# Attention in a hand-given order over head pairs, two heads next to each other on the PE array

## The chip, the cores and the metric

The kernel runs on one core of one Trainium2 chip. The core has five engines with queues of their own: PE (matmul, with its weight loads shown apart as PEld), DVE (vector), ACT (scalar functions), POOL and SP. SP and POOL issue most of the transfers; 16 DMA engines carry them out. The metric is the device time of one execution in microseconds (us), lower is better.

## The reference

Attention of 8 batches with 12 heads, 448 tokens and 64 columns a head; its output, 3584 tokens of 768 columns, goes through a mixture of 8 experts of which each keeps its 80 best tokens.

```python
# attention
rms = sqrt(mean(x * x, axis=-1, keepdims=True) + 1e-06)     # for q and for k
q_n, k_n = q / rms * g_q, k / rms * g_k
scores = 1/sqrt(64) * matmul(q_n, k_n.transpose(0, 1, 3, 2))
attn = exp(scores - max); attn = attn / (sum(attn, axis=-1) + 1e-09)
o = matmul(attn, v)                      # (8, 12, 448, 64) -> x (3584, 768)
# experts
logits = x @ w_gate                      # (3584, 8)
expert_idx = argmax(logits); gate_w = softmax(logits)[expert_idx]
for e in range(8):
    tok_idx = the 80 tokens of expert e with the largest gate_w
    h = maximum(x[tok_idx] @ w1[e], 0.0)                    # 768 -> 1024
    out[tok_idx] = gate_w[tok_idx, None] * (h @ w2[e])      # 1024 -> 768
```

All other rows of the output are zero.

## The kernel before

The kernel works on pairs of heads (`HP = 2`). For a pair q, k and v are loaded as four tiles of 112 tokens. Squares, their sums (L111, L114), a root on ACT (L117) and a reciprocal (L120) give the scale of each token; L127 and L130 apply it. Transposes on PE (L141, L143) put both heads' columns on the partitions, head 0 on 0 to 63 and head 1 on 64 to 127 (`qnT`, `knT`). Then the heads are taken one after the other. For each tile j of 112 keys a score matmul (L160) uses 64 rows of the array and ACT takes the exp (L163). Four AV matmuls (L168) accumulate in one PSUM tile `po`. `v_sb` has a 65th column of ones, so that row 64 of `po` is the sum of the exps. That row is copied (L172), moved to partition 0 by a transfer, spread over 64 partitions by POOL (L176), inverted (L177) and multiplied into the output (L179), which goes to DRAM as `xT_b`.

After each batch the gate reads `xT_b` back in four tiles of tokens (`gxT`), transposes it to tokens on partitions, casts it to bf16 and writes it to `xbf_scratch`; six matmuls (L202) make the logits, from which the score of each token for its expert goes to `S_sb`. The order of the instructions in this part is the scheduler's: the code above is written batch by batch, and the engines' queues come out interleaved.

At the end 10 rounds of three DVE instructions over 8 x 3584 (L240, L242, L246) find the 80 best tokens of each expert. For each expert POOL gathers their rows (L261), and loads w1 and w2 (L274, L278, 1536 KB each, two buffers); PE transposes (L269) and multiplies (L287, L299), and POOL scatters the result (L306). All of these transfers stand in POOL's queue. The output's 28 blocks of zeros are written by SP before anything is loaded (L74):

```python
    for i in range(N // 128):
        nc.sync.dma_start(out=out[i * 128:(i + 1) * 128, :], in_=zeros[:, :])
```

Of the kernel before, what the change touches and what calls it, by code (L numbers as in the profile page):

```python
# [14 lines left out]
U32 = mybir.dt.uint32  # L16


@with_exitstack
def kernel(  # L20
# [21 lines left out]

    ST = 112
    NT = S // ST
    HP = 2
    DC = DM // 128
    FC = F // 128

    xTd = [nc.dram_tensor(f"xT_b{b}", (DM, S), F32, kind="Internal").ap()
           for b in range(B)]  # L50
# [6 lines left out]
    ident = cpool.tile([128, 128], F32)  # L57
    make_identity(nc, ident[:, :])
    identb = cpool.tile([128, 128], BF16)
    nc.vector.tensor_copy(identb[:, :], ident[:, :])  # L60

    gq_sb = cpool.tile([D, 1], F32)
    gk_sb = cpool.tile([D, 1], F32)
    nc.sync.dma_start(out=gq_sb[:, :], in_=g_q[:, None])
    nc.sync.dma_start(out=gk_sb[:, :], in_=g_k[:, None])
    gqk = cpool.tile([HP * D, 1], F32)
    nc.vector.tensor_mul(gqk[:D, :], gq_sb[:, :], gk_sb[:, :])
    nc.vector.tensor_scalar_mul(gqk[:D, :], gqk[:D, :], 1.0 / math.sqrt(D))
    nc.gpsimd.tensor_copy(gqk[D:2 * D, :], gqk[:D, :])

    zeros = cpool.tile([128, DM], F32)
    nc.vector.memset(zeros[:, :], 0.0)
    for i in range(N // 128):
        nc.sync.dma_start(out=out[i * 128:(i + 1) * 128, :], in_=zeros[:, :])  # L74

    S_sb = cpool.tile([E, N], F32)
    wg_sb = cpool.tile([128, DC, E], F32)
    nc.sync.dma_start(out=wg_sb[:, :, :],
                      in_=moe_w_gate.rearrange("(c p) e -> p c e", p=128))

    with tc.tile_pool(name="attn_sb", bufs=3) as spool, \
         tc.tile_pool(name="attn_ps", bufs=2, space=bass.MemoryType.PSUM) as ppool, \
         tc.tile_pool(name="attn_tps", bufs=2, space=bass.MemoryType.PSUM) as tps, \
         tc.tile_pool(name="attn_big", bufs=2) as bpool, \
         tc.tile_pool(name="gate_sb", bufs=3) as gsb, \
         tc.tile_pool(name="gate_ps", bufs=2, space=bass.MemoryType.PSUM) as gps:

        def attention_batch(b):
            for hp in range(H // HP):
                h0 = hp * HP  # L90
                q_sb = spool.tile([ST, NT, HP, D], F32, tag="q", name="q_sb")
                k_sb = spool.tile([ST, NT, HP, D], F32, tag="k", name="k_sb")
                v_sb = spool.tile([ST, NT, HP, D + 1], F32, tag="v",
                                  name="v_sb")
                nc.gpsimd.memset(v_sb[:, :, :, :], 1.0)
                for hh in range(HP):
                    h = h0 + hh
                    nc.sync.dma_start(
                        out=q_sb[:, :, hh, :],
                        in_=q[b, h].rearrange("(t p) d -> p t d", p=ST))  # L100
                    nc.sync.dma_start(
                        out=k_sb[:, :, hh, :],
                        in_=k[b, h].rearrange("(t p) d -> p t d", p=ST))
                    nc.sync.dma_start(
                        out=v_sb[:, :, hh, :D],
                        in_=v[b, h].rearrange("(t p) d -> p t d", p=ST))

                def rms_scale(src, name):
                    sq = spool.tile([ST, NT, HP, D], F32, tag=name + "sq",
                                    name=name + "sq")  # L110
                    nc.vector.tensor_mul(sq[:], src[:], src[:])  # L111
                    ssq = spool.tile([ST, NT, HP], F32, tag=name + "ssq",
                                     name=name + "ssq")
                    nc.vector.reduce_sum(out=ssq[:], in_=sq[:], axis=AX.X)  # L114
                    nc.vector.tensor_scalar(ssq[:], ssq[:], 1.0 / D, 1e-6,
                                            op0=ALU.mult, op1=ALU.add)
                    nc.scalar.sqrt(ssq[:], ssq[:])  # L117
                    rstd = spool.tile([ST, NT, HP], F32, tag=name + "rstd",
                                      name=name + "rstd")
                    nc.vector.reciprocal(rstd[:], ssq[:])  # L120
                    return rstd

                q_rstd = rms_scale(q_sb, "q")
                k_rstd = rms_scale(k_sb, "k")
                for t in range(NT):
                    for hh in range(HP):
                        nc.vector.tensor_scalar(  # L127
                            q_sb[:, t, hh, :], q_sb[:, t, hh, :],
                            q_rstd[:, t, hh:hh + 1], None, op0=ALU.mult)
                        nc.vector.tensor_scalar(  # L130
                            k_sb[:, t, hh, :], k_sb[:, t, hh, :],
                            k_rstd[:, t, hh:hh + 1], None, op0=ALU.mult)

                qnT = bpool.tile([HP * D, S], F32, tag="qnT", name="qnT")
                knT = bpool.tile([HP * D, S], F32, tag="knT", name="knT")
                for t in range(NT):
                    pq = tps.tile([HP * D, ST], F32, space=bass.MemoryType.PSUM, tag="transp",
                                  name="pq")
                    pk = tps.tile([HP * D, ST], F32, space=bass.MemoryType.PSUM, tag="transp",
                                  name="pk")  # L140
                    nc.tensor.transpose(pq[:, :], q_sb[:, t, :, :],  # L141
                                        ident[:ST, :ST])
                    nc.tensor.transpose(pk[:, :], k_sb[:, t, :, :],  # L143
                                        ident[:ST, :ST])
                    nc.vector.tensor_scalar(qnT[:, t * ST:(t + 1) * ST],  # L145
                                            pq[:, :], gqk[:, :], None,
                                            op0=ALU.mult)
                    nc.vector.tensor_copy(knT[:, t * ST:(t + 1) * ST],  # L148
                                          pk[:, :])

                for hh in range(HP):
                    h = h0 + hh
                    qT_h = qnT[hh * D:(hh + 1) * D, :]
                    kT_h = knT[hh * D:(hh + 1) * D, :]
                    attnT = [bpool.tile([ST, S], F32, tag=f"attnT{j}",
                                        name=f"attnT{j}") for j in range(NT)]
                    for j in range(NT):
                        ps = ppool.tile([ST, S], F32, space=bass.MemoryType.PSUM,
                                        tag="score", name="ps")
# [5 lines left out]
                    po = ppool.tile([D + 1, S], F32, space=bass.MemoryType.PSUM, tag="outT",  # L165
                                    name="po")
                    for j in range(NT):
                        nc.tensor.matmul(po[:, :], v_sb[:, j, hh, :],  # L168
                                         attnT[j][:, :],
                                         start=(j == 0), stop=(j == NT - 1))  # L170
                    zrow = spool.tile([D + 1, S], F32, tag="zrow", name="zrow")
                    nc.vector.tensor_copy(zrow[D:D + 1, :], po[D:D + 1, :])  # L172
                    zrow0 = spool.tile([1, S], F32, tag="zrow0", name="zrow0")
                    nc.sync.dma_start(out=zrow0[:, :], in_=zrow[D:D + 1, :])
                    zb = spool.tile([D, S], F32, tag="zb", name="zb")
                    nc.gpsimd.partition_broadcast(zb[:, :], zrow0[:, :])  # L176
                    nc.vector.reciprocal(zb[:, :], zb[:, :])  # L177
                    xT = spool.tile([D, S], F32, tag="xT", name="xT")
                    nc.vector.tensor_mul(xT[:, :], po[:D, :], zb[:, :])  # L179
                    nc.sync.dma_start(out=xTd[b][h * D:(h + 1) * D, :],  # L180
                                      in_=xT[:, :])

        def gate_tile(b, ti, ntok):
            xT = gsb.tile([128, DC, 128], F32, tag="gxT", name="gxT")
            nc.sync.dma_start(
                out=xT[:, :, :ntok],
# [158 lines left out]
```

## Time and profile before

| | |
|---|---|
| runs shown | 1396.58, 1398.98, 1406.75 us (median 1398.98) |
| profiled execution, span | 1407.2 us |
| mean granted clock of TensorE in it | 0.772 of 2.4 GHz |
| busy in it | PE 1042.4, PEld 423.1, DVE 969.9, ACT 476.5, POOL 130.1 us |
| moved | 100.69 MB |

The profiled execution is one of the program on the chip; its span runs from the first to the last instruction. The busy times of engines overlap, and those of PE are modelled at their ends. The granted clock is 1.0 at 2.4 GHz and 0.5 at 1.2 GHz; values between are means over a stretch.

### The profile page before, as it was taken

The numbers are of one execution on the slowest core, as the hardware profiler recorded it, in microseconds if no ns is written. First come the engines' busy times: TensorE is split into PE (matmuls) and PEld (weight loads), VectorE is DVE, ScalarE is ACT, GpSimd is POOL, SyncE is SP. The second block draws the span as 40 slices with busy tenths as digits, with TensorE's granted clock in tenths as the row PEclk, the third lists the DMA queues.
The fourth block names the chain that finished last, engine by engine and source line by source line (L and its number), as shares of the span: only waits on it lengthen the run. The fifth ranks groups of instructions, "written<-read, shape, count | busy, mean of one in ns | idle before, by whom it ended". The sixth has DMA issues, their size and how long they took to land. (4 is left out here: it accounts for less than half of the span.)

```text
span 1407.2 us, 11745 instructions
## 1 busy us (share of the span) xinstructions
PE 1042.4 (74%) x3088; PEld 423.1 (30%) x3088; DVE 969.9 (69%) x2386; ACT 476.5 (34%) x758; POOL 130.1 (9%) x183
## 2 busy tenths in 40 slices
PE   0889899899989998999898899989997130004544
PEld 0333234333333433333333233333332120003433
DVE  0887777877598668868877887698685159992110
ACT  0453433553265335534543543365241000000100
POOL 0000000100011000100010010001000100002121
PEclk9987787887588678979888878889798555556666
DMA  9321232223123212312232123123200930006997
GB/s 334 75 47 36 50 81 58 52 67 68 33 53 73 62 30 53 93 43 53 46 84 56 41 49 94 42 53 79 56 20 14 187 54 0 0 0 124 175 185 139
DMA packets 216147, 100.69 MB, mean 72 GB/s; under 512 B 172944, under 2 KB 205712, under 8 KB 216080
## 3 DMA queue, kind: packets, MB, share of 16 engines
q1 hardware_dynamic: 200592, 71.82, 21.1%
q0 software_dynamic: 15488, 28.12, 10.8%
q8 instruction: 25, 0.41, 0.1%
q14 instruction: 42, 0.34, 0.1%
HBM read 95.39 MB, written 29.50 MB: 89 GB/s over the span
## 5 line engine op out<-in xcount | busy, mean ns | idle before, releaser
L160 PE MATMUL ps<-qnT,knT 64*112 64x448 f32 x768 | 424.8, 680 | 8.6 <-DVE qnT L145 4.0
L168 PE MATMUL po<-attnT,v_sb 112*65 112x448 f32 x768 | 400.1, 658 | 10.3 <-ACT attnT L163 10.3
L163 ACT ACTIVATE attnT<-ps 112x448 f32<-112x448 f32 x384 | 202.0, 542 | 358.3 <-PE ps L160 356.4
L177 DVE RECIPROCAL zb<-zb 64x448 f32<-64x448 f32 x96 | 281.7, 2934 | 9.0 <-POOL zb L176 9.0
L160 PEld LDWEIGHTS ps<-qnT,knT 64*112 64x112 f32 x768 | 135.1, 203 | 198.7 <-issue 116.4
L168 PEld LDWEIGHTS po<-attnT,v_sb 112*65 112x65 f32 x768 | 111.9, 163 | 253.6 <-issue 213.4
L163 ACT ACT_TABLE_LOAD x91 | 116.8, 1283 | 100.8 <-PE ps L160 99.7
L176 POOL PARTITION_BROADCAST zb<-zrow x96 | 73.9, 769 | 761.3 <-DMA zrow<-zrow 494.7
L172 DVE COPY zrow<-po 1x448 f32<-1x448 f32 x96 | 59.7, 622 | 106.1 <-PE po L168 104.6
L141 PE MATMUL pq<-ident,q_sb 112*128 112x112 f32 x192 | 62.4, 325 | 89.8 <-DVE qnT L145 50.7
L269 PE MATMUL pxt<-identb,xg 80*128 80x80 bf16 x48 | 8.4, 226 | 152.2 <-DMA xg<-xbf_scratch,idx_e 148.6
L117 ACT ACT_TABLE_LOAD x91 | 116.8, 1283 | 2.3 <-PEq L326 0.7
L196 DVE CAST xbf<-pt 128x128 bf16<-128x128 f32 (+1 forms) x192 | 48.3, 272 | 74.9 <-PE pt L193 47.8
L291 ACT ACTIVATE h_sb<-ph 128x80 bf16<-128x80 f32 x64 | 14.5, 237 | 230.3 <-PE ph L287 230.1
L130 DVE TENSOR_SCALAR k_sb<-k_sb,krstd 112x64 f32<-112x64 f32 x384 | 92.1, 274 | 0.2
L127 DVE TENSOR_SCALAR q_sb<-q_sb,qrstd 112x64 f32<-112x64 f32 x384 | 85.1, 263 | 0.2
L193 PE MATMUL pt<-ident,gxT 128*128 128x128 f32 (+1 forms) x192 | 54.6, 337 | 39.2 <-DVE xbf L196 25.7
L141 PEld LDWEIGHTS pq<-ident,q_sb 112*128 112x128 f32 x192 | 29.8, 155 | 154.1 <-DVE qnT L145 74.2
L145 DVE TENSOR_SCALAR qnT<-pq,gqk 128x112 f32<-128x112 f32 x192 | 61.1, 318 | 17.1 <-PE pq L141 13.6
L143 PE MATMUL pk<-ident,k_sb 112*128 112x112 f32 x192 | 59.0, 308 | 17.3 <-DVE knT L148 16.3
L302 DVE TENSOR_SCALAR yo<-py,gw_e 80x384 f32<-80x384 f32 x16 | 9.8, 612 | 85.6 <-PE py L299 83.5
L211 ACT ACTIVATE lex<-lex 128x8 f32<-128x8 f32 (+1 forms) x32 | 6.7, 209 | 171.6 <-DVE lex L209 171.5
(55 smaller groups left out, 808.9 us busy)
## 6 DMA issues: line engine op xcount, KB each, us to landing
w_sb<-in_moe_w_dram POOLq DMA_DIRECT2D x16, 1536.0 KB, 15.6
out_dram<-zeros SPq DMA_DIRECT2D x28, 384.0 KB, 4.0
q_sb<-in_q_dram SPq DMA_DIRECT2D x96, 112.0 KB, 2.6
k_sb<-in_k_dram SPq DMA_DIRECT2D x96, 112.0 KB, 2.7
v_sb<-in_v_dram SPq DMA_DIRECT2D x96, 112.0 KB, 2.5
xT_b<-xT SPq DMA_DIRECT2D x96, 112.0 KB, 2.2
gxT<-xT_b SPq DMA_DIRECT2D x24, 384.0 KB, 4.6
xbf_scratch<-xbf SPq DMA_DIRECT2D x144, 32.0 KB, 1.5
```

The costliest lines, as they stand in the source:

```text
L117: nc.scalar.sqrt(ssq[:], ssq[:])
L127: nc.vector.tensor_scalar(q_sb[:, t, hh, :], q_sb[:, t, hh, :], q_rstd[:, t, hh:hh + 1], None, op0=ALU.mult)
L130: nc.vector.tensor_scalar(k_sb[:, t, hh, :], k_sb[:, t, hh, :], k_rstd[:, t, hh:hh + 1], None, op0=ALU.mult)
L141: nc.tensor.transpose(pq[:, :], q_sb[:, t, :, :], ident[:ST, :ST])
L143: nc.tensor.transpose(pk[:, :], k_sb[:, t, :, :], ident[:ST, :ST])
L145: nc.vector.tensor_scalar(qnT[:, t * ST:(t + 1) * ST], pq[:, :], gqk[:, :], None, op0=ALU.mult)
L160: nc.tensor.matmul(ps[:, :], kT_h[:, j * ST:(j + 1) * ST], qT_h[:, :], start=True, stop=True)
L163: nc.scalar.activation(attnT[j][:, :], ps[:, :], AF.Exp)
L168: nc.tensor.matmul(po[:, :], v_sb[:, j, hh, :], attnT[j][:, :], start=(j == 0), stop=(j == NT - 1))
L172: nc.vector.tensor_copy(zrow[D:D + 1, :], po[D:D + 1, :])
L176: nc.gpsimd.partition_broadcast(zb[:, :], zrow0[:, :])
L177: nc.vector.reciprocal(zb[:, :], zb[:, :])
```

## The change

The 48 pairs of all batches become steps of one loop (`for n in range(-4, NP + 6)`), in an order that is written out by hand (`manual_schedule`) and is kept by every engine. In step n the scores of pair n, AV of pair n - 1, the transposes of pair n + 1, the normalisation of pair n + 2 and the squares of pair n + 3 stand interleaved. The two heads' matmuls of a key tile stand next to each other: scores on rows 0 to 63 and 64 to 127, AV on columns 0 to 63 and 64 to 127 of one accumulator `po` (one buffer). The exp takes both heads at once. The column of ones goes; DVE adds the four exp tiles (`presum`), and for every second pair `zl` multiplies the sums with a selector and the unnormalised outputs `us` with the gate's weights, into one PSUM bank for a batch: 32 columns of the array for each of four heads. Some steps later `gate1`, `gate2` and `xout` transpose, divide, and write `xbf_scratch` once a batch; `xT_b` and its way through DRAM are gone. Square moves to ACT, the root becomes a power on POOL. The zero blocks are written in the loop, one for every second step. The weights of experts 0 and 1 are loaded in the loop; those of experts 2 to 6 have buffers of their own, in space that the attention's pools had, and expert 7 takes expert 2's. The expert loop keeps its matmuls; PSUM is read in larger pieces, and a gather has three buffers.

```diff
-                        nc.tensor.matmul(ps[:, :],
-                                         kT_h[:, j * ST:(j + 1) * ST],
-                                         qT_h[:, :], start=True, stop=True)
-                        nc.scalar.activation(attnT[j][:, :], ps[:, :], AF.Exp)
...
+        def square(n):
+            sq = prep.tile([ST, 2 * 2 * NT * D], F32, tag="sq", name="sq", bufs=1)
+            nc.scalar.activation(sq[:, :], st[n]["qk"][:].rearrange("p a h x -> p (a h x)"),
+                                 AF.Square)
...
+        def rstd(n):
+            ssq = prep.tile([ST, 16], F32, tag="ssq", name="ssq")
+            nc.vector.reduce_sum(out=ssq[:, :], in_=st[n]["sq"][:].rearrange(
+                "p (g d) -> p g d", d=D), axis=AX.X)
...
+            nc.gpsimd.tensor_tensor(rs[:].rearrange("p a h j -> p (a h j)"), ms[:, :],
+                                    nhalf[:, :], op=ALU.pow)
...
+        def transp(n, a):
+            tp = tpps.tile([128, 512], F32, tag="tp", name="tp")
+            for j in range(NT):
+                nc.tensor.transpose(tp[:, j * ST:(j + 1) * ST],
+                                    st[n]["qn"][:, a, j].rearrange("p h d -> p (h d)"),
+                                    ident[:ST, :ST])
...
+        def score(n, j):
...
+            ps = scps.tile([ST, 2, 512], F32, tag="sc", name="ps")
+            for hh in range(2):
+                nc.tensor.matmul(ps[:, hh, :S],
+                                 st[n]["T1"][hh * D:(hh + 1) * D, j * ST:(j + 1) * ST],
+                                 st[n]["T0"][hh * D:(hh + 1) * D, :],
+                                 start=True, stop=True)
+            nc.scalar.activation(st[n]["at"][:, j], ps[:, :, :S], AF.Exp)
+
+        def av(n, j):
+            if j == 0:
+                st[n]["po"] = pops.tile([128, 512], F32, tag="po", name="po")
+            for hh in range(2):
+                nc.tensor.matmul(st[n]["po"][hh * D:(hh + 1) * D, :S],
+                                 st[n]["v"][:, hh, j * D:(j + 1) * D],
+                                 st[n]["at"][:, j, hh, :],
+                                 start=(j == 0), stop=(j == NT - 1))
...
+        def presum(n):
...
+            nc.vector.tensor_add(t0[:], at[:, 0], at[:, 1])
+            nc.vector.tensor_add(t1[:], at[:, 2], at[:, 3])
+            nc.vector.tensor_add(sm[:], t0[:], t1[:])
...
+        def uevac(n):
+            us = upool.tile([128, S], F32, tag="us", name="us")
+            nc.vector.tensor_copy(us[:, :], st[n]["po"][:, :S])
...
+        def zl(n):
...
+                nc.tensor.matmul(t[32 * c:32 * c + 32, :S], zsel[:, i, :],
+                                 st[m]["sm"][:, c % 2, :], start=(i == 0), stop=False)
...
+                nc.tensor.matmul(t[32 * c:32 * c + 32, :S], wgs[:, 4 * i + c, :],
+                                 st[m]["us"][:, :], start=False, stop=(i == NG - 1))
...
+        for n in range(-4, NP + 6):
+            if ok(n + 4):
+                load_qk(n + 4)
+            if ok(n + 2):
+                load_v(n + 2)
+            if n >= 0 and n % 2 == 0 and n // 2 < N // 128:
+                i = n // 2
+                nc.sync.dma_start(out=out[i * 128:(i + 1) * 128, :], in_=zeros[:, :])
+            if n >= 2 and n % 6 == 2 and n // 6 < NW0:
+                fetch_w1(n // 6)
...
+            if ok(n):
+                score(n, 0)
+            if ok(n - 2):
+                uevac(n - 2)
+            if ok(n - 1):
+                av(n - 1, 0)
+                presum(n - 1)
+            if ok(n + 1):
+                transp(n + 1, 0)
+            if ok(n):
+                score(n, 1)
+            if ok(n - 1):
+                av(n - 1, 1)
+            if ok(n - 2) and (n - 2) % 2 == 1:
+                zl(n - 2)
+            if ok(n + 2):
+                normalise(n + 2)
...
+            if ok(n + 3):
+                square(n + 3)
+                rstd(n + 3)
+            if ok(n - 1):
+                av(n - 1, 3)
...
+        for e in range(NW0, E):
+            load_weights(wlate, e)
+            fetch_w1(e)
+            fetch_w2(e)
         for e in range(E):
```

PE's queue of the kernel before, in the middle of the attention; `ps` are the scores of one head, `po` its AV, `pq` and `pk` the transposes.

```order
L160 MATMUL ps<-qnT,knT 112x448 x2
L168 MATMUL po<-attnT_5847,v_sb 65x448
L168 MATMUL po<-attnT_5848,v_sb 65x448
L168 MATMUL po<-attnT_5849,v_sb 65x448
L168 MATMUL po<-attnT_5850,v_sb 65x448
L160 MATMUL ps<-qnT,knT 112x448 x2
L141 MATMUL pq<-ident,q_sb 128x112
L143 MATMUL pk<-ident,k_sb 128x112
```

PE's queue of the changed kernel for one pair with `zl`; each x2 of L189 (scores) and L199 (AV) is the two heads of a key tile.

```order
L189 MATMUL ps<-qkT 112x448 x2
L199 MATMUL po<-at,vt 64x448 x2
L174 MATMUL tp<-ident,qn 128x112 x4
L189 MATMUL ps<-qkT 112x448 x2
L199 MATMUL po<-at,vt 64x448 x2
L228 MATMUL zl<-sm,zsel 32x448 x4
L232 MATMUL zl<-us,wgs 32x448 x4
L189 MATMUL ps<-qkT 112x448 x2
L199 MATMUL po<-at,vt 64x448 x2
L174 MATMUL tp<-ident,qn 128x112 x4
L189 MATMUL ps<-qkT 112x448 x2
L199 MATMUL po<-at,vt 64x448 x2
```

Runs of one head's matmuls have become an alternation of score and AV, each for two heads.

DVE's queue of the changed kernel, from one copy of `po` (L216) to the next.

```order
L216 COPY us<-po 128x448
L209 TENSOR_TENSOR t_2784<-at 112x896
L210 TENSOR_TENSOR t_2785<-at 112x896
L211 TENSOR_TENSOR sm<-t_2784,t_2785 112x896 [waits DVE_49]
L165 TENSOR_TENSOR qn<-qk,rs 112x2x4x64 [waits DMAHW5_49,Pool_49]
L165 TENSOR_TENSOR qn<-qk,rs 112x2x4x64 [waits DMAHW6_49]
L151 TENSOR_REDUCE ssq<-sq 112x16 [waits Activation_49]
L289 TENSOR_TENSOR xb<-xp,rz 112x4x128 [waits PE_49] x2
L216 COPY us<-po 128x448
```

In DVE's queue of the kernel before, a head's row of sums and output are handled between other heads' work.

```order
L177 RECIPROCAL zb<-zb 64x448 [waits Pool_49]
L196 CAST xbf<-pt 128x128 [waits DMAHW1_49,PE_49]
L196 CAST xbf<-pt 128x128 [waits DMAHW2_49,PE_49]
L179 TENSOR_TENSOR xT<-po,zb 64x448 [waits DVE_49]
L196 CAST xbf<-pt 128x128 [waits DMAHW3_49,PE_49]
```

The reciprocals over 448 columns are gone, and the reduce L151, which waits for ACT's Square, now stands between the copies of `po`.

POOL's queue of the kernel before, from the last broadcast on; L274 and L278 load weights, L261 gathers, L306 scatters.

```order
L176 ISA zb<-zrow_7903 64x448
L274 DMA w_sb<-in_moe_w_dram 128x6x1024
L278 DMA w_sb<-in_moe_w_dram 128x8x768
L274 DMA w_sb<-in_moe_w_dram 128x6x1024
L278 DMA w_sb<-in_moe_w_dram 128x8x768
L261 DMA xg<-xbf_scratch,idx_e 80x768 x2
L274 DMA w_sb<-in_moe_w_dram 128x6x1024
```

POOL's queue of the changed kernel at its end; L102 and L106 load weights, L392 gathers, L426 scatters.

```order
L106 DMA w_sb<-in_moe_w_dram 128x8x768
L102 DMA w_sb<-in_moe_w_dram 128x6x1024 [waits DMASW4_49]
L106 DMA w_sb<-in_moe_w_dram 128x8x768 [waits DMASW5_49]
L392 DMA xg<-xbf_scratch,idx_e 80x768 [waits DMAHW0_49,DMASW6_49,DVE_49]
L392 DMA xg<-xbf_scratch,idx_e 80x768 [waits DMAHW2_49,DMASW7_49,DVE_49]
L392 DMA xg<-xbf_scratch,idx_e 80x768 [waits DMAHW4_49,DMASW0_49,DVE_49]
```

Ten weight loads (experts 2 to 6) now stand ahead of the first gather, where four stood; four others (experts 0 and 1) have moved into the attention.

## Rows read from the trace of the kernel before

**Rows 1.** Stages: us, busy PE, PEld, DVE, ACT, POOL (count), clock, DMA share, GB/s.

```profile
0.00:44.00 44.00, 2.52 (x8) 1.42 (x8) 9.85 (x39) 2.27 (x5) 2.40 (x10) 1.00 0.88 298
44.00:1082.00 1038.00, 949.49 (x2437) 359.45 (x2438) 804.34 (x2157) 458.47 (x686) 97.02 (x140) 0.82 0.24 55
1082.00:1148.40 66.40, 23.06 (x84) 14.19 (x82) 19.09 (x58) 1.26 (x5) 4.47 (x5) 0.54 0.69 130
1148.40:1264.40 116.00, 0.00 (x0) 0.00 (x0) 115.30 (x71) 0.00 (x0) 0.00 (x0) 0.50 0.00 0
1264.40:1407.20 142.80, 67.36 (x560) 48.08 (x560) 21.35 (x65) 14.46 (x64) 26.22 (x28) 0.66 0.84 154
```

**Rows 2.** Groups of 44 to 1082 us: busy us, mean ns, idle before.

```profile
L160 PE MATMUL ps<-qnT,knT 64*112 64x448 f32 x768 | 424.8, 680 | 8.6 <-DVE qnT L145 4.0 <-ACT attnT L163 3.5
L168 PE MATMUL po<-attnT,v_sb 112*65 112x448 f32 x761 | 397.5, 659 | 10.3 <-ACT attnT L163 10.3
L177 DVE RECIPROCAL zb<-zb 64x448 f32<-64x448 f32 x95 | 278.7, 2934 | 7.0 <-POOL zb L176 7.0
L163 ACT ACTIVATE attnT<-ps 112x448 f32<-112x448 f32 x384 | 202.0, 542 | 358.3 <-PE ps L160 356.4
...
L172 DVE COPY zrow<-po 1x448 f32<-1x448 f32 x95 | 59.1, 622 | 105.7 <-PE po L168 104.2
...
L111 DVE TENSOR_TENSOR ksq<-k_sb 112x512 f32<-112x512 f32 x47 | 32.0, 681 | 0.0
L114 DVE TENSOR_REDUCE kssq<-ksq 112x8 f32<-112x512 f32 x47 | 31.5, 670 | 0.2
...
L117 ACT ACTIVATE kssq<-kssq 112x8 f32<-112x8 f32 x47 | 9.8, 208 | 3.6 <-DVE kssq L115 3.2
```

**Rows 3.** Timeline of PEld, full clock: start us, us, instruction, idle before.

```profile
1080.84 0.27 PEld L160 LDWEIGHTS ps<-qnT,knT 64*112 64x112 f32 x2 [0.48 <-ACT attnT L163]
1081.77 0.19 PEld L168 LDWEIGHTS po<-attnT,v_sb 112*65 112x65 f32 x2 [0.66 <-PE ps L160]
1082.20 0.14 PEld L168 LDWEIGHTS po<-attnT,v_sb 112*65 112x65 f32 x1 [0.24 <-issue]
1082.58 0.14 PEld L168 LDWEIGHTS po<-attnT,v_sb 112*65 112x65 f32 x1 [0.24 <-issue]
```

**Rows 4.** Timeline of PEld at the lower clock.

```profile
424.32 0.23 PEld L168 LDWEIGHTS po<-attnT,v_sb 112*65 112x65 f32 x1 [0.51 <-issue]
425.07 0.23 PEld L168 LDWEIGHTS po<-attnT,v_sb 112*65 112x65 f32 x1 [0.52 <-issue]
```

**Rows 5.** Timeline of PE, two transposes.

```profile
440.82 0.26 PE L141 MATMUL pq<-ident,q_sb 112*128 112x112 f32 x1
440.92 0.26 PE L143 MATMUL pk<-ident,k_sb 112*128 112x112 f32 x1
```

**Rows 6.** Two stretches of 4 us, columns as in rows 1.

```profile
412.00:416.00 4.00, 1.11 (x4) 0.72 (x4) 3.73 (x9) 0.21 (x2) 0.86 (x2) 0.81 0.36 82
416.00:420.00 4.00, 3.73 (x7) 1.35 (x6) 4.00 (x9) 1.64 (x2) 0.24 (x1) 0.50 0.53 121
```

**Rows 7.** Timeline of SP's queue, the first load of q.

```profile
29.51 1.19 SPq L98 DMA_DIRECT2D q_sb<-in_q_dram  x1
```

**Rows 8.** Timeline of PEld, the drain.

```profile
1097.89 0.29 PEld L193 LDWEIGHTS pt<-ident,gxT 128*128 128x128 f32 x2 [13.67 <-DMA gxT<-xT_b]
```

**Rows 9.** Experts: transfers (KB, median us to landing), a stretch, two rows of PE.

```profile
idx_e<-idx_scratch SPq DMA_DIRECT2D x8, 0.3 KB, 5.1
out_dram<-yo,idx_e POOLq DMA_INDIRECT x8, 8.3
...
1278.00:1394.00 116.00, 56.66 (x485) 40.79 (x484) 14.88 (x53) 12.78 (x57) 23.29 (x25) 0.68 1.02 184
...
1280.13 0.24 PE L269 MATMUL pxt<-identb,xg 80*128 80x80 bf16 x2
...
1283.94 2.44 PE L299 MATMUL py<-w_sb,h_sb 128*80 128x384 bf16 x14
```

More of the change, by code (lines that the diff above doesn't have):

```diff
@@ L44 @@
     NT = S // ST
-    HP = 2
+    HP = H // 2
+    NP = B * HP
     DC = DM // 128
     FC = F // 128
-    xTd = [nc.dram_tensor(f"xT_b{b}", (DM, S), F32, kind="Internal").ap()
-           for b in range(B)]
+    NG = H // 4
     xbf_dram = nc.dram_tensor("xbf_scratch", (N, DM), BF16, kind="Internal").ap()
@@ L66 @@
[L66 to L71, printed above, removed]
-    nc.vector.memset(zeros[:, :], 0.0)
[L73 to L77, printed above, removed]
@@ new lines @@
+    gk2 = cpool.tile([128, 2], F32, name="gk2")
+    for half in range(2):
+        nc.sync.dma_start(out=gk2[half * D:(half + 1) * D, 0:1], in_=g_q[:, None])
+        nc.sync.dma_start(out=gk2[half * D:(half + 1) * D, 1:2], in_=g_k[:, None])
+    gqk = cpool.tile([128, 1], F32, name="gqk")
+    nc.vector.tensor_mul(gqk[:, :], gk2[:, 0:1], gk2[:, 1:2])
+    nc.vector.tensor_scalar_mul(gqk[:, :], gqk[:, :], 1.0 / math.sqrt(D))
+    zsel = cpool.tile([ST, NG, 32], F32, name="zsel")
+    nc.vector.memset(zsel[:, :, :], 0.0)
@@ new lines @@
+    for i in range(NG):
+        nc.vector.memset(zsel[:, i, 24 + i:25 + i], 1.0)
+    wgs = cpool.tile([128, H, 32], F32, name="wgs")
+    nc.vector.memset(wgs[:, :, :], 0.0)
+    wg_v = moe_w_gate.rearrange("(i c hh d) e -> hh d i c e", hh=2, c=2, d=D)
+    for hh in range(2):
+        for i in range(NG):
+            nc.sync.dma_start(
+                out=wgs[hh * D:(hh + 1) * D, 4 * i + hh:4 * i + hh + 3:2, 8 * i:8 * i + 8],
+                in_=wg_v[hh, :, i])
+    nhalf = cpool.tile([ST, 16], F32, name="nhalf")
@@ L283 @@
-            for fc in range(FC):
-                ph = mps.tile([128, CAP], F32, space=bass.MemoryType.PSUM, tag="ph",
-                              name="ph")
-                for c in range(DC):
-                    nc.tensor.matmul(ph[:, :],
-                                     w1_sb[:, c, fc * 128:(fc + 1) * 128],
-                                     xgT[:, c, :],
-                                     start=(c == 0), stop=(c == DC - 1))
-                nc.scalar.activation(h_sb[:, fc, :], ph[:, :], AF.Relu)
+                out=xg[:, :], out_offset=None, in_=xbf_dram[:, :],
@@ new lines @@
+            h_sb = mpool.tile([128, FC, CAP], BF16, tag="hsb", name="h_sb")
+            for fh in range(2):
+                ph = mps.tile([128, FC // 2, CAP], F32, tag="ph", name="ph")
+                for f4 in range(FC // 2):
+                    fc = fh * (FC // 2) + f4
+                    for c in range(DC):
+                        nc.tensor.matmul(ph[:, f4, :],
+                                         w1_sb[:, c, fc * 128:(fc + 1) * 128],
+                                         xgT[:, c, :],
+                                         start=(c == 0), stop=(c == DC - 1))
+                nc.scalar.activation(h_sb[:, fh * (FC // 2):(fh + 1) * (FC // 2), :],
+                                     ph[:], AF.Relu)
```

387 lines of the change are left out of this document (201 added, 186 removed).

## The prediction

> **What bounds the kernel now.** I read the stages first. Their rows [rows 1] cut the 1407.2 us of the profiled execution into a head without matmuls to speak of (44 us), the attention (1038 us for 48 pairs of heads, 21.6 us a pair), a drain with the last batch's gate (66 us), the top-k passes (116 us) and the experts (143 us). In the attention PE is busy 949 of 1038 us, DVE 804, ACT 458, so PE is the bound there, with DVE close behind. In the drain and the top-k no matmul matters, and in the experts the DMA share is 0.84 with PE at 67 of 143 us. So the attention must be priced in PE passes, the other stages by what ends last in each.
>
> The groups of the attention [rows 2] say what the passes are: scores 768 and AV 768 (two passes for each of the 384 matmuls), 825 of 949 us busy. The count is per head: a head uses 64 rows of the array for a score and 65 columns for AV. Because "busy" overlaps in a pipeline, I take the price of a pass from starts of weight loads instead. In a run of AV passes at full clock they start 0.376 us apart, 1082.20 to 1082.58 [rows 3]. Where a score pair is followed by AV the two passes take 0.93 us, 1080.84 to 1081.77, so a change of the form of the matmul costs 0.18 there; the first AV pass takes 0.43, or 0.05 more. At the lower clock, 1.2 GHz, a pass takes 0.75 us [rows 4]. Transposes of 112 columns start 0.10 us apart [rows 5]. The mean granted clock of the attention is 0.82 [rows 1]. It falls where PE has stood idle: in 412 to 416 us PE is busy 1.11 of 4 us, and in the four us behind it the clock is 0.50 though PE is busy 3.73 of 4 [rows 6].
>
> **The change, part by part.** *Scores and AV.* A pair still has 8 score and 8 AV matmuls of two passes and 448 columns, but the two heads of a step now stand next to each other, on rows 0 to 63 and 64 to 127 for scores, and on columns 0 to 63 and 64 to 127 for AV. No place of the trace of before has two matmuls on different tiles next to each other, so the price of such a pair must be bounded: two slots if both run fully side by side, four if not at all. I take three. PE issues in program order, first head pass 1, pass 2, second head pass 1, pass 2; pass 2 of a head needs the same rows as its pass 1, so it starts one slot later [rows 3], and only the second head's pass 1 can lie beside it. That is nearest to the one fact shown, that passes on the same rows follow each other at 0.376. Then a score step costs 3 x 0.376 + 0.18 = 1.31 us and a pair 5.2; an AV step, with a change that I put at 0.14 (between 0.05 and 0.18), 1.27 and a pair 5.1.
>
> *Transposes.* 8 a pair as before, in two blocks of 4: 0.8 us by [rows 5] and 0.2 for each change of form, 1.2. *Row sums and gate logits.* The 65th column of ones goes, as do the per-head RECIPROCAL of 2934 ns, its broadcast and the copy of a row [rows 2]. Instead there are 8 matmuls for two pairs, 32 columns of the array each. By the same staggering 16 passes take 9 slots, 3.4 us, so 1.75 a pair. The 4 output transposes of a pair take 0.5. Sum on PE: 5.2 + 5.1 + 1.2 + 1.75 + 0.5 = 13.8 us a pair at full clock. At the clock of before, 0.82, that is 16.8.
>
> *Waits between engines.* There is one AV accumulator, so the first AV step of a pair waits until DVE has copied out the last one. On DVE that copy stands behind the reduce of squares, which waits for the Square on ACT, which stands behind the last exp. From the end of the last score step the chain is: an exp of 896 columns, 0.88 us (542 ns for 448 and 208 for 8 give 0.75 ns a column [rows 2]); a Square of 1024 columns, 0.98 at the same rate; a reduce of 1024 elements, under twice the 670 ns of 512, 1.2; a copy of 448 columns, 0.62; about 0.2 for hand-overs: 3.9 us. Against it PE has one AV and one score step, 2.6 us. The stall is 1.3 us a pair at full clock and nothing at 1.2 GHz, where PE takes 5.1; I count 0.7. It could be 0, if the gate's work between two pairs covers it, or 1.3. The gate of a batch adds some ten short DVE instructions and six multiplications of 512 columns at about 0.68 [rows 2], some 6 us a batch, 1 us a pair; nothing if hidden, 1.3 if not at all. A pair: 16.8 + 0.7 + 1.0 = 18.5 us, the attention 48 x 18.5 = 888.
>
> *DVE and ACT* are not the bound: DVE has per pair three additions of 896 columns (1.2 each, by 681 for 512), two multiplications (0.7), the reduce (1.2) and the copy (0.6), 6.8 us; ACT four exps, two copies of 448 (0.54) and the Square, 5.6. If PE shared fully, they would still be under its 10 us.
>
> *Head.* The 28 zero fills leave the front of SP's queue, where the first load of q is issued at 29.51 [rows 7] and the first score at 44.0. Ten small transfers stay ahead of it; at 1.19 us each, as the row shows for q's issue, they would take 12, and I take half: 6 + 14.5 = 20 us in place of 44. The fills now go out one for every two pairs, between loads needed three to four pairs later; the DMA share there is 0.24 [rows 1], so I cost them, and the four weight loads of experts 0 and 1 that POOL issues there, at nothing. If that cover were gone, four loads at 8 us would cost 32.
>
> *Drain.* The way through DRAM goes: PE waits 13.67 us for its first tile [rows 8], and PE is busy only 23 of 66 us [rows 1]. What is left behind the last score is AV of the last pair (5.1 / 0.82 = 6), its sums and logits (3.4 / 0.82 = 4), and the gate's ten short DVE instructions and six multiplications with their hand-overs (an estimate, 12): 22 in place of 66. *Top-k.* 29 of 30 passes over 3584 columns remain: 116 x 29 / 30 = 112.
>
> *Experts.* Here the change costs time. Before, four weight loads were underway before the top-k; 12 followed. Now four are done in the attention, but the other loads stand on POOL ahead of the gathers, and their buffers are those of the attention's pools, so the first waits until the top-k has ended and the index writes have landed (4 us, under the 5.1 of the read back [rows 9]). A load is 1536 KB, which at 184 to 206 GB/s (the row 1278 to 1394 gives 184 [rows 9]) is 7.6 to 8.5 us; I take 8. The ten loads end 84 us behind the top-k; only then come the gathers, and PE, which had two experts' weights all along, begins at 87. An expert takes 6.3 us (1280.13 to 1283.94 + 2.44 [rows 9]). Expert 2's first half ends at about 103 and frees the buffer of expert 7's weights, 16 us more, 119; the gather of expert 4 stands behind these on POOL, 122; four experts, 25, and the last scatter's landing, 8.3 [rows 9]: 155 in place of 143.
>
> **Sum.** 20 + 888 + 22 + 112 + 155 = 1197 us against the span of 1407.2. The median of the runs shown, 1398.98, is 0.6% under that span, so 1197 becomes **1190**.
>
> **The rivals.**
> *Full sharing:* the two heads of a step run side by side in two slots. For it: rows and columns are disjoint. Against: two passes of each, issued in order. A pair: score steps 0.93 and AV steps 0.89, 7.3; transposes 1.2, sums 0.8, output 0.5: 9.8, at 0.82 12.0, with the gate 1.0 and the stall, now longer, 1.6: 14.6 x 48 = 701, plus 309: 1010, about 1005. The Trainium skill, "TensorE: Matmul & The Clock Gate", section "Measured speedup vs the span model", gives the span of packed tiles as about that of one matmul with a few ns for each further tile; by that rule this rival is the time. No run here shows it.
> *No sharing,* the change doing not what it says: 4 slots a step, 6.7 + 6.6 + 1.2 + 3.0 + 0.5 = 18.1. At full clock with gate and stall 19.7 a pair, 946 + 309, about 1250; at 0.82 23.3, about 1420; in the middle 1330. For it: nothing in the trace shows two tiles at work at once.
> *Full clock with sharing:* 13.8 + 1.3 + 1.0 = 16.1 a pair, 773 + 309, about 1075. For it: the order leaves PE fewer and shorter waits. Against: a stall of 1.3 us a pair stays, and the clock of before fell behind waits [rows 6].
> *The clock stays at 1.2 GHz:* short waits at every pair and the changes of form keep it down. A pass then takes 0.75 [rows 4], a pair 27.4 + 1.0, the attention 1363, the whole about 1660, slower than before. It decides where 13.8 / clock + 1.7 passes (1407 - 309) / 48 = 22.9 us, at a mean clock under 0.65. For it: drain and experts of before ran at 0.50 to 0.66 [rows 1]. Against: the attention, with longer waits than those to come, kept 0.82.
>
> **How the numbers follow.** Chances: the forecast with sharing in three slots and a clock near 0.82, 0.45; full sharing 0.15; full clock 0.12; no sharing 0.20, a quarter of it slower than before; the low clock 0.08. The forecast alone, with its bounds (stall 0 to 1.3, gate 0 to 1.3, clock 0.78 to 0.88, experts 143 to 165), spans 1130 to 1250. For 8 in 10 the range takes in the full-clock case, half of the full sharing and most of no sharing: 1020 to 1400; outside are the low clock and the ends, together under 0.2. A change within 1%, which is about what a measurement of this kernel can tell from none, needs one narrow stretch of the no-sharing case: 0.03. Slower by over 1%: 0.08 + 0.04 = 0.12. Faster: 0.85.
>
> **What the profile after would show.** Right: in a score step the weight loads of the four passes start so that the step takes 1.3 us at full clock, not 0.9 or 1.7; 18 to 19 us a pair; a wait of about 1 us of the first AV step for DVE's copy; first score at about 20 us; a MoE stage that is longer than before, with PE idle for some 85 us behind the top-k while weights come. I would be wrong if steps take two or four slots, if the clock of the attention leaves 0.78 to 0.88, if the gathers pass the weight loads in the queue, or if DVE, not PE, sets the pace.

## The result and the profile after

The changed kernel takes 963.2 us (962.13 to 969.48, four runs) against 1399.62 for the kernel before: the ratio is 0.6877, 95% interval 0.6842 to 0.6913. The forecast was 1190 with a range from 1020; the kernel is faster than the whole range. The profiled execution has a span of 960.3 us at a mean clock of 0.803.

The stages of the changed kernel, columns as in [rows 1]: head, attention (first to last score), drain, top-k, experts.

```profile
0.00:21.50 21.50, 1.75 (x8) 1.41 (x8) 5.40 (x14) 4.58 (x6) 4.33 (x10) 1.00 0.35 83
21.50:676.40 654.90, 537.03 (x2488) 179.19 (x2488) 340.07 (x467) 274.87 (x339) 150.69 (x97) 0.88 0.29 82
676.40:694.25 17.85, 11.82 (x68) 6.07 (x64) 12.88 (x25) 0.76 (x2) 0.00 (x0) 0.81 0.00 0
694.25:809.00 114.75, 0.00 (x0) 0.00 (x0) 113.79 (x50) 0.00 (x0) 0.00 (x0) 0.50 0.03 9
809.00:960.30 151.30, 43.64 (x560) 34.22 (x560) 16.02 (x36) 7.00 (x16) 25.92 (x28) 0.66 0.77 145
```

Four of the five stages came out near their terms: 21.5 (forecast 20), 17.9 (22), 114.8 (112) and 151.3 (155), together 305 for 309. The error lies in the attention: 655 us, 13.6 a pair, for 888. The groups of its 655 us answer to [rows 2]; the last number before an arrow is the engine's idle time ahead of the group:

```profile
L189 PE MATMUL ps<-qkT 64*112 64x448 f32 x768 | 224.4, 666 | 0.6 <-ACT qkT L181 0.6
L199 PE MATMUL po<-at,vt 112*64 112x448 f32 x752 | 202.6, 619 | 64.1 <-DVE us L216 34.3 <-issue 25.6 <-PE ps L189 4.2
L193 ACT ACTIVATE at<-ps 112x896 f32<-112x896 f32 x192 | 176.1, 917 | 231.8 <-PE ps L189 231.8
...
L151 DVE TENSOR_REDUCE ssq<-sq 112x16 f32<-112x1024 f32 x46 | 56.1, 1220 | 270.4 <-ACT sq L145 270.4
...
L145 ACT ACTIVATE sq<-qk 112x1024 f32<-112x1024 f32 x46 | 48.3, 1049 | 0.0
...
L276 PE MATMUL sp<-ident,sc 112*8 112x112 f32 x28 | 6.4, 381 | 30.9 <-DVE sc L273 30.9
L240 PE MATMUL zt<-ident,zsb 128*112 128x128 f32 x28 | 4.5, 285 | 19.9 <-DVE zsb L237 19.9
```

The counts of passes are those of before (768 and 768, some records missing), but the busy time has halved: 224 for 425 us, 203 for 398. Weight loads of the changed kernel, as in [rows 3], show one score step, one AV step and one block of transposes:

```profile
409.72 0.27 PEld L189 LDWEIGHTS ps<-qkT 64*112 64x112 f32 x4 [0.70 <-issue]
410.66 0.20 PEld L199 LDWEIGHTS po<-at,vt 112*64 112x64 f32 x4 [0.67 <-issue]
411.56 0.39 PEld L174 LDWEIGHTS tp<-ident,qn 112*128 112x128 f32 x4 [0.70 <-issue]
```

A score step takes 0.94 us and an AV step 0.90: two slots (a slot is the 0.376 us of one pass) and a change of form each, not three slots. Inside the score step the four weight loads lie within 0.27 us.

PE is idle for 118 of the 655 us, in the places that were named: 64.1 ahead of AV and 51 ahead of the gate's transposes (L276, L240). The timeline of PE at the first AV step of a pair, that of DVE ahead of it, and two stretches of 4 us around it:

```profile
401.71 1.01 PE L189 MATMUL ps<-qkT 64*112 64x448 f32 x4
404.86 1.55 PE L199 MATMUL po<-at,vt 112*64 112x448 f32 x4 [2.14 <-issue]
406.34 1.01 PE L174 MATMUL tp<-ident,qn 112*128 112x112 f32 x4
407.28 1.61 PE L189 MATMUL ps<-qkT 64*112 64x448 f32 x4
```

```profile
401.81 1.22 DVE L151 TENSOR_REDUCE ssq<-sq 112x16 f32<-112x1024 f32 x1 [6.32 <-ACT sq L145]
402.94 1.28 DVE L289 TENSOR_TENSOR xb<-xp,rz 112x512 bf16<-112x512 f32 x2
404.14 0.61 DVE L216 COPY us<-po 128x448 f32<-128x448 f32 x1
```

```profile
401.00:405.00 4.00, 1.86 (x14) 0.98 (x13) 3.19 (x5) 1.69 (x2) 1.80 (x2) 1.00 0.00 0
405.00:409.00 4.00, 4.00 (x14) 1.36 (x14) 3.96 (x5) 0.70 (x2) 1.30 (x1) 0.57 0.00 0
```

AV waits 2.14 us, and behind the wait the granted clock is 0.57: the next score step takes 1.5 us instead of 0.94. The wait is put down to "issue", but DVE's copy L216 ran from 404.14 to 404.75, just ahead of AV's start at 404.86. Two of the gate's multiplications (L289) stand between the reduce and the copy here and make 1.28 us of the chain.

In the experts' stage POOL's timeline has the first weight load and the first gather, and PE's the first matmul:

```profile
811.61 0.89 POOL L102 DMA_DIRECT2D w_sb<-in_moe_w_dram  x1 [168.89 <-DMA gw_scratch<-gw_all]
...
839.22 1.06 POOL L392 DMA_INDIRECT xg<-xbf_scratch,idx_e  x1 [7.13 <-DMA w_sb<-in_moe_w_dram]
...
891.31 0.96 PE L398 MATMUL pxt<-identb,xg 80*128 80x80 bf16 x12 [197.70 <-DMA xg<-xbf_scratch,idx_e]
```

The gather is issued at 839.22, but PE gets its rows only at 891.31, 82 us behind the end of the top-k, when the loads ahead of it are in (forecast 87).

### The profile page after: what moved, and what is told of

Read it like the earlier page. It is cut to its first block, busy times and chain, and to the rows that moved or that the text cites. A ratio compares the mean times of both kernels' runs of the same rounds, so it can differ in the third digit from the quotient of the medians.

```text
span 960.3 us, 7959 instructions
## 1 busy us (share of the span) xinstructions
PE 594.2 (62%) x3120; PEld 220.9 (23%) x3120; DVE 488.1 (51%) x589; ACT 287.2 (30%) x361; POOL 180.9 (19%) x134
## 4 chain that ended last, share of the span: by engine, by line
PE 48%; another core or an unknown queue 21%; DVE 11%; issue 7%; DMA 6%; ACT 4%; SPq 1%; POOL 1%; POOLq 0%; ACTq 0%; DVEq 0%
PE ps L189 18%; PE po L199 15%; PE tp L174 5%; DVE ssq L151 4%; ACT sq L145 4%; DMA out_dram<-yo,idx_e 3%; PE xp L285 3%; DMA vt<-in_v_dram 3%; PE zl L228 2%; PE zl L232 2%; DVE us L216 1%; DVE qn L165 1%; PE ph L409 1%; DVE S_sb L277 1%
## 5 line engine op out<-in xcount | busy, mean ns | idle before, releaser
L199 PE MATMUL po<-at,vt 112*64 112x448 f32 x768 | 205.8, 618 | 64.8 <-DVE us L216 35.0
L193 ACT ACTIVATE at<-ps 112x896 f32<-112x896 f32 x192 | 176.1, 917 | 231.8 <-PE ps L189 231.8
L189 PE MATMUL ps<-qkT 64*112 64x448 f32 x768 | 224.4, 666 | 0.6 <-ACT qkT L181 0.6
L151 DVE TENSOR_REDUCE ssq<-sq 112x16 f32<-112x1024 f32 x48 | 58.5, 1220 | 278.7 <-ACT sq L145 278.7
L157 POOL TENSOR_TENSOR rs<-ms,nhalf 112x16 f32<-112x16 f32 x48 | 140.1, 2918 | 4.0
L199 PEld LDWEIGHTS po<-at,vt 112*64 112x64 f32 x768 | 41.9, 146 | 216.8 <-issue 144.8
L174 PE MATMUL tp<-ident,qn 112*128 112x112 f32 x384 | 65.8, 301 | 20.8 <-DVE qn L165 20.8
L189 PEld LDWEIGHTS ps<-qkT 64*112 64x112 f32 x768 | 59.4, 192 | 77.8 <-issue 48.0
L165 DVE TENSOR_TENSOR qn<-qk,rs 112x512 f32<-112x512 f32 x96 | 61.8, 685 | 11.7 <-POOL rs L157 11.7
L211 DVE TENSOR_TENSOR sm<-t,t 112x896 f32<-112x896 f32 x48 | 52.4, 1092 | 1.7
L209 DVE TENSOR_TENSOR t<-at 112x896 f32<-112x896 f32 x48 | 52.2, 1087 | 0.0
L210 DVE TENSOR_TENSOR t<-at 112x896 f32<-112x896 f32 x48 | 51.9, 1082 | 0.0
L102 POOL DMA_DIRECT2D w_sb<-in_moe_w_dram x8 | 7.2, 897 | 175.2 <-DMA gw_scratch<-gw_all 168.9
L289 DVE TENSOR_TENSOR xb<-xp,rz 112x512 bf16<-112x512 f32 x48 | 31.7, 686 | 16.8 <-PE xp L285 16.5
```

Of the source, the lines that this page charges most:

```text
L151: nc.vector.reduce_sum(out=ssq[:, :], in_=st[n]["sq"][:].rearrange("p (g d) -> p g d", d=D), axis=AX.X)
L157: nc.gpsimd.tensor_tensor(rs[:].rearrange("p a h j -> p (a h j)"), ms[:, :], nhalf[:, :], op=ALU.pow)
L165: nc.vector.tensor_mul(qn[:, a].rearrange("p j h d -> p h j d"), qk[:, a].rearrange("p h (j d) -> p h j d", d=D), rs[:, a].unsqueeze(3).to ...
L174: nc.tensor.transpose(tp[:, j * ST:(j + 1) * ST], st[n]["qn"][:, a, j].rearrange("p h d -> p (h d)"), ident[:ST, :ST])
L189: nc.tensor.matmul(ps[:, hh, :S], st[n]["T1"][hh * D:(hh + 1) * D, j * ST:(j + 1) * ST], st[n]["T0"][hh * D:(hh + 1) * D, :], start=True, ...
L193: nc.scalar.activation(st[n]["at"][:, j], ps[:, :, :S], AF.Exp)
```

## The experiments

Each run was timed beside the kernel before on its chip (medians 1403.4 to 1406.4). Times are medians unless the text says otherwise. Sharing is that the two heads' passes lie side by side in the array.

**Sharing undone for scores.** Head 1's scores are computed from head 0's q and k.

```diff
-    st[n]["T1"][hh * D:(hh + 1) * D, j * ST:(j + 1) * ST],
-    st[n]["T0"][hh * D:(hh + 1) * D, :],
+    st[n]["T1"][:D, j * ST:(j + 1) * ST],
+    st[n]["T0"][:D, :],
```

> The changed kernel, but the score matmuls of both heads read rows 0 to 63 (head 1's scores are computed from head 0's q and k). The instructions, their sizes and their order stay; only the scores of a step no longer lie on different rows. Theory (the gain came from two heads running fully side by side): a score step grows from two slots, 0.94 us, to four, 1.68, so 3.0 us a pair at full clock, 3.4 at the clock of 0.88; some of it is taken back where PE waits for the copy of the AV accumulator anyway: 1060 to 1125 us in place of 963. Rival (sharing is not what counts, PE would wait for DVE and ACT all the same): under 1000 us. Rival (two passes of a head are the unit, and the two slots come from something else than disjoint rows): 963 us, unchanged.

**Sharing undone for AV.** Each AV matmul takes 128 columns of v and accumulates into all partitions.

```diff
-    nc.tensor.matmul(st[n]["po"][hh * D:(hh + 1) * D, :S],
-                     st[n]["v"][:, hh, j * D:(j + 1) * D],
+    nc.tensor.matmul(st[n]["po"][:, :S],
+                     st[n]["v"][:, hh, j * D:j * D + 128] if j < 3
+                     else st[n]["v"][:, hh, 128:256],
```

> The changed kernel, but each AV matmul takes 128 columns of v as weights in place of 64 and both heads accumulate into all 128 partitions (the output is then not attention's). The number of passes and their 448 streamed columns stay; the two heads no longer lie on different columns. Theory (full side by side): an AV step grows from 0.90 to 1.65 us, 3.0 us a pair, the same 1060 to 1125 us as without sharing of the scores. Rival (PE would wait anyway): under 1000 us.

Measured: 1259.89 us without sharing of scores in the shortest of four runs, 297 us above the changed kernel (median 1285.5, longest 1297.1; the profile is of the longest), and 1032.2 without that of AV. The attention's stretch, first of the kernel with scores on the same rows, then of the one with AV on all columns:

```profile
21.30:1015.90 994.60, 929.15 (x2488) 311.27 (x2488) 340.17 (x468) 275.81 (x339) 150.54 (x97) 0.68 0.19 54
```

```profile
21.70:747.30 725.60, 639.73 (x2485) 272.55 (x2486) 339.80 (x467) 275.42 (x340) 150.72 (x97) 0.95 0.26 74
```

Both steps grew to four slots (at full clock 1.68 us for scores, 396.97 to 398.65 on PE's timeline; AV 1.61 or 1.70, to the transposes or to the sums behind it). But neither time came out as expected. With AV the attention grew by 71 us, half of the 144 that 3.0 us a pair make: PE's idle time fell from 118 to 86 us and the clock rose from 0.88 to 0.95. With scores it grew by 340 us in the profiled run, more than double, at a clock of 0.68, although PE was idle less (65 us) than in the changed kernel. Over the whole execution the mean clock was 0.672 in this run and 0.698 in the shortest, for 0.803 in the changed kernel. So waits alone do not account for the clock.

**Scores on all rows.** To part the slots from the clock, each score matmul takes all 128 rows; both then compute the sum of the heads' scores.

```diff
+    st[n]["T1"][:, j * ST:(j + 1) * ST],
+    st[n]["T0"][:, :],
```

> The changed kernel, but each of the two score matmuls of a step uses all 128 rows (both heads' columns at once, so both compute the sum of the two heads' scores). Four slots a step as with both heads on rows 0 to 63, which took 1285 us at a clock of 0.68 in the attention; only the rows in use differ. Theory (two effects there: 3.0 us a pair for the slots, and a clock that fell because half of the array's rows lay idle): the slots are lost and the clock holds above 0.9, as with AV on all columns: 1030 to 1070 us. Rival (the slots or the longer step are the cause of the low clock): 1200 us or more.

Measured: 1020.28 us. The attention:

```profile
21.20:732.20 711.00, 618.99 (x2486) 235.91 (x2488) 339.95 (x467) 275.00 (x340) 150.60 (x97) 0.95 0.27 75
```

The same four slots, and the clock at 0.95 in place of 0.68. The slots cost 56 us of attention net, with the waits that they cover. What scores on 64 rows, one head behind the other, cost beyond that is 240 us by the shortest run (1259.89 to 1020.28) and 284 in the profiled one. The form of the matmul is not the cause: the changed kernel's scores have the same 64 rows a matmul, on both halves side by side, and ran at 0.88.

**The same in the kernel before.** Its score matmuls, one head on 64 rows, are given all 128.

```diff
-                    qT_h = qnT[hh * D:(hh + 1) * D, :]
-                    kT_h = knT[hh * D:(hh + 1) * D, :]
+                    qT_h = qnT[:, :]
+                    kT_h = knT[:, :]
```

> The kernel before, but each score matmul uses all 128 rows of qnT and knT (the sum of both heads' scores) in place of one head's 64. Passes, order and waits stay. Theory (half-empty rows also held down the clock of the kernel before, 0.82 in the attention): the clock of the attention rises, to 0.9 or more, and the attention shortens by 50 to 100 us: 1300 to 1350 us. Rival (there the clock fell behind waits alone, as the prediction read it): within 1% of the kernel before.

Measured: 1270.23 us, ratio 0.9048 (0.901 to 0.9087). The attention of this kernel:

```profile
43.80:941.00 897.20, 782.18 (x2438) 346.07 (x2439) 805.03 (x2158) 457.75 (x686) 96.68 (x140) 0.94 0.28 64
```

It is 141 us shorter than in [rows 1], with the same passes and the same DVE work, at a clock of 0.94 for 0.82, although PE was idle longer (115 us for 89). The low clock of the kernel before was for the most part not due to its waits.

**Order of the heads.** On top of the kernel with the copy first (below), AV of two key tiles stands together, once with alternating heads, once with the heads apart.

```diff
+            for jj, hh in ((j - 1, 0), (j - 1, 1), (j, 0), (j, 1)):
+            for jj, hh in ((j - 1, 0), (j, 0), (j - 1, 1), (j, 1)):
```

> The kernel with the copy ahead of the reduce (816 us), AV of two key tiles at a time, the heads alternating: head 0 and 1 of tile j - 1, then head 0 and 1 of tile j. One group of 4 matmuls replaces two groups of 2, so two changes of form a pair fewer each way. Both theories: four slots for a group, 1.65 us in place of 2 x 0.90, 0.3 us a pair: 795 to 816 us.

> As the kernel with alternating heads, but head 0's two key tiles first, then head 1's two. Theory (what the prediction assumed: passes start in the order of the program, one column half at a time): head 1's first pass can lie beside head 0's last one only, seven slots in place of four, 1.13 us a group, 2.3 us a pair, 108 us more at full clock: 900 to 930 us. Rival (matmuls of different tiles are taken out of order, as the first passes of both heads that start 7 ns apart suggest): within 1% of the alternating kernel.

Measured: 798.17 and 799.62 us. Weight loads of the kernel with the heads apart, one group of AV and the sums behind it:

```profile
402.76 0.20 PEld L201 LDWEIGHTS po<-at,vt 112*64 112x64 f32 x4 [0.67 <-DVE ssq L151]
403.19 0.15 PEld L201 LDWEIGHTS po<-at,vt 112*64 112x64 f32 x2 [0.23 <-issue]
403.56 0.15 PEld L201 LDWEIGHTS po<-at,vt 112*64 112x64 f32 x2 [0.23 <-issue]
404.42 0.16 PEld L230 LDWEIGHTS zl<-sm,zsel 112*32 112x32 f32 x8 [0.70 <-issue]
```

The group takes 1.66 us, four slots and a change of form; behind the first four the loads come in twos, 0.37 us apart. The rows do not name the head, but passes on the same columns took a slot each (AV on all columns), so two that start together must be one of each head, although the program has both matmuls of head 0 first. Matmuls on different columns were not held to the program's order.

**One part alone in the kernel before.** For each key tile both heads' scores, then both exps. The edit moves more than that: AV of both heads now stands behind all scores of the pair, where head 0's AV stood ahead of head 1's scores, and the scheduler's order follows.

> The kernel before with one part of the change alone: the scores of both heads of a pair stand next to each other for each key tile (rows 0 to 63 and 64 to 127); AV, row sums, gate, transfers and the scheduler's order stay. Theory (sharing alone frees PE, and PE was the bound): a pair's 16 score passes take 8 slots, 3.0 us a pair at full clock, 3.7 at 0.82; DVE, 16.8 us a pair, is not reached: 1220 to 1260 us. Rival (two score buffers and DVE's 804 of 1038 us take the place of PE): 1340 us or more.

Measured: 1635.38 us, ratio 1.1626 (1.1587 to 1.1665): slower than before. The attention, a piece of PE's timeline in it, and the groups of PE with the most idle time ahead of them:

```profile
44.00:1303.00 1259.00, 938.88 (x2428) 363.64 (x2428) 807.68 (x2155) 410.60 (x657) 91.83 (x139) 0.71 0.20 45
```

```profile
619.72 1.44 PE L159 MATMUL ps<-qnT,knT 64*112 64x448 f32 x4 [0.69 <-ACT attnT L164]
621.35 1.44 PE L159 MATMUL ps<-qnT,knT 64*112 64x448 f32 x4 [0.20 <-ACT attnT L164]
```

```profile
L159 PE MATMUL ps<-qnT,knT 64*112 64x448 f32 x768 | 395.4, 868 | 118.9 <-DVE qnT L145 73.3 <-ACT attnT L164 44.9
...
L141 PE MATMUL pq<-ident,q_sb 112*128 112x112 f32 x188 | 65.9, 350 | 81.5 <-DVE qnT L145 81.5
L143 PE MATMUL pk<-ident,k_sb 112*128 112x112 f32 x188 | 64.0, 340 | 63.1 <-DVE knT L148 61.4
...
L229 PE MATMUL pst<-ident,sc 128*8 128x128 f32 x28 | 9.2, 329 | 44.5 <-DVE sc L224 44.5
```

Four passes do run as a step, but the steps start 1.63 us apart: with two score buffers the next pair waits for both exps (two of 541 ns) and the hand-overs. PE has no AV in between to fill the gap here. It is idle for 320 of 1259 us, for 89 before, and the clock is 0.71. Of this idle time 45 us wait for the exps, which free the score buffers, but 261 us in these rows wait for DVE. So both parts of the rival came true, and DVE's was the larger. What the sharing itself saved was not parted from the new order.

**The copy ahead of the reduce.** The reduce of squares and the power move one step later, behind `uevac` and the first AV step.

```diff
             if ok(n - 1):
                 av(n - 1, 0)
+            if ok(n + 2):
+                rstd(n + 2)
+            if ok(n - 1):
                 presum(n - 1)
...
                 square(n + 3)
-                rstd(n + 3)
```

> The changed kernel with one move on DVE and POOL: the reduce of squares and the power stand one step later, behind the copy of the AV accumulator, so that this copy no longer waits for Square on ACT. Theory (the stall of the first AV step is the chain exp, Square, reduce, copy): the 35 us that AV waits for the copy and most of the 26 us behind it go, the clock falls less often, 900 to 930 us in place of 963. Rival (the copy then waits for something else as late, or normalise waits for POOL's power of 2.9 us): 950 us or more.

Measured: 816.02 us, ratio to before 0.581 (0.5785 to 0.5836), 147 us below the changed kernel. The attention:

```profile
21.20:539.50 518.30, 483.83 (x2488) 164.31 (x2488) 343.54 (x467) 274.23 (x339) 215.95 (x97) 0.97 0.37 103
```

PE's groups of this kernel, for those with idle time above:

```profile
L199 PE MATMUL po<-at,vt 112*64 112x448 f32 x752 | 186.6, 574 | 16.5 <-PE ps L189 15.0 <-DVE us L216 1.4
...
L276 PE MATMUL sp<-ident,sc 112*8 112x112 f32 x28 | 4.1, 274 | 12.9 <-DVE sc L273 12.9
```

The expected 900 to 930 missed by far. PE's idle time in the attention fell from 118 to 34 us: 48 ahead of AV, where I had expected it, and 38 ahead of the gate's transposes, where I had not (L240 waits no more). PE's busy time fell by another 53 us for the same passes, at a clock of 0.97 for 0.88. So the time gained, 137 us, was more than the idle time removed.

**Weights beside the top-k.** The pools of the attention close ahead of the top-k passes, whose small tiles move to the constants' pool; the loads stand ahead of them; expert 7 takes expert 0's buffers.

```diff
-        slot = e if e < NW0 else NW0 + (e - NW0) % 5
+        slot = e if e < E - 1 else 0
...
+        with tc.manual_schedule():
+            for e in range(NW0, E - 1):
+                load_weights(wlate, e)
+                fetch_w1(e)
+                fetch_w2(e)
...
```

> The changed kernel with the attention's pools closed ahead of the top-k passes, so that the weights of experts 2 to 6 load beside them; expert 7's go into expert 0's buffers. Theory (the experts' stage is 151 us because ten loads of 8 us begin only behind the top-k and stand ahead of the gathers): the stage becomes about 4 + 3 + 8 x 6.3 + 8 = 65 us, the whole 870 to 890 us. Rival (loads beside the top-k slow DVE's passes down, or the gathers wait for something else): over 900 us.

> The changed kernel with both moves at once: the reduce of squares behind the copy of the AV accumulator, and the attention's pools closed ahead of the top-k with the weights of experts 2 to 6 beside it. Theory (the two pay in different stages): 816 less the 80 us of the second move, 735 to 740 us. Rival (they share a cause, or the load of the DMA engines moves into the attention's end): 755 us or more.

> The kernel with both moves (738 us) and AV of two key tiles at a time with alternating heads. Theory (0.3 us a pair for changes of form, as 816 to 798 showed): 718 to 726 us. Rival (the end of the chain is elsewhere by now): 738 us.

Measured: 883.08, 738.18 and 721.51 us. Top-k and experts of the kernel with this move alone:

```profile
692.25:810.80 118.55, 4.29 (x19) 2.85 (x18) 117.67 (x60) 0.00 (x0) 8.59 (x10) 0.51 0.75 142
810.80:885.70 74.90, 46.00 (x560) 36.29 (x560) 14.53 (x30) 7.00 (x16) 17.31 (x18) 0.80 0.39 83
```

The experts' stage halves, from 151 to 75 us, and the loads cost the top-k nothing that shows: it and the drain together take 132 us as before the move. The moves add up (147 and 80 together 225), and AV in groups gives 17 more. The last kernel, with all of them, has a ratio to before of 0.5131 (0.5098 to 0.5165).

**Zeros first.** The 28 fills go back ahead of the first loads.

> The changed kernel with the 28 zero blocks written ahead of the first load of q and k, as before. Theory (the head shrank because SP's queue was cleared): the first score moves from 21.5 to about 46 us, the whole to 985 to 990 us. Rival (the fills inside the attention cost about as much there): 963 us, unchanged.

Measured: 990.22 us. The first score starts at 48.7 us in place of 21.5, and the attention behind it has the same length, 654.4 us and clock 0.88: the fills inside the loop cost nothing there.

## Why the prediction was wrong

**The step that failed** is the choice of three slots: "pass 2 of a head needs the same rows as its pass 1, so it starts one slot later [rows 3], and only the second head's pass 1 can lie beside it". Its premise, that PE issues in program order, does not hold between tiles on different columns: heads apart and heads alternating take the same time. For scores, on different rows, the order was not varied; there the four weight loads of a step come together. Both kinds of step take two slots. At the steps' 0.94 and 0.90, transposes of 0.53 a block, half of 1.6 for the sums and 0.5 for the output transposes, a pair is 9.7 us at full clock, about the 9.8 of the rival with full sharing, not 13.8. That rival gave 1005. The rule of the Trainium skill named there ("TensorE: Matmul & The Clock Gate", "Measured speedup vs the span model") agrees with the trace: a score step takes 0.94 us for two heads against 0.93 for one [rows 3].

**The clock** was carried over at 0.82. It was 0.88, the upper end of its bounds. The view behind it, that it falls behind waits [rows 6], was only a part of the matter: in the kernel before it was 0.94 in place of 0.82 once the scores took all 128 rows. In the changed kernel the two heads of a step lie on all rows together, so the change can gain in slots and in clock. That is why the measured attention, 13.6 us a pair, is under the rival's 14.6, which kept 0.82.

In the sum's own terms: two slots in place of three take 240 us from the 888 (4.1 a pair at 0.82), the clock 39 more, and the waits, 2.46 us a pair (118 / 48) for 0.7 + 1.0, add 36. That makes 645 for the measured 655. The forecast's range by its own bounds was also too narrow: all low ends together give about 1043 and all high ends 1285, not 1130 and 1250. Even 1043 is above 963.

**Right in place, by luck in size:** the chain behind the AV accumulator. AV's idle time, 64.1 us over 48 pairs, is 1.3 a pair, and the chain was put at 1.3 at full clock, of which 0.7 was counted. But that 1.3 was 3.9 less 2.6 us for two steps of three slots. With the measured steps, 1.84 us, it would be 2.1, as in the piece of timeline above (2.14, there with the gate's multiplications in the way). Its price is open: the copy experiment took 137 us out of the attention, but the gate's waits fell with it, and the two were not parted.

**Right in place and size:** the gate's waits (51 us, 1.1 a pair, for 1.0); the head; the experts' stage with its ten loads, PE's first matmul 82 us behind the top-k; DVE and ACT not the bound (340 and 275 of 655 us). The drain was 4 us shorter than I put it.

**The other rivals:** no sharing and a clock that stays at half are excluded for this kernel, by steps of two slots and a clock of 0.88. The full clock came in part, but on steps of two slots, not the three of that rival; with the copy first it was 0.97. A low clock has its place elsewhere: 0.68 in the profiled run with scores on the same rows, 0.71 in the kernel before with the heads adjacent.

## What to carry to other kernels

Put small matmuls that use different rows or columns of the array next to each other, and count such a group as one, but only when the engines around it keep up (here ACT, with one exp for both heads and a buffer in hand, and DVE, with its order written out); put into the kernel before, with its two score buffers and its queue on DVE, the adjacent heads made it slower. Price a wait of the bound engine at more than its length, by the clock in the rows behind it. When a pool's release decides when a load may start, look at which long stage without transfers it could lie beside.

## What the runs showed of the hardware

In one program with the same passes the mean granted clock of the attention was 0.68 with scores on 64 rows, one head after the other (the longest of four runs; the shortest had 0.698 over the whole execution, for 0.858 with 128 rows), and 0.95 with scores on 128 rows, though PE was busy more of the time in the first (929 of 995 us, 619 of 711). In the kernel before the same swap gave 0.82 and 0.94. What in the rows' use the clock follows was not settled; the values that are multiplied differ between these runs too, and that was not parted.

Two fp32 matmuls of two passes and 448 columns took 0.94 us on two halves of the rows and 0.90 on two halves of the columns, as one score matmul alone took (0.93 [rows 3]). On the same rows or the same columns they took 1.68 and 1.61 to 1.70.
